# Reordering the opening and the first weight products of a fused FFT and GeGLU kernel on one core

## The chip, the core and the metric

The kernel runs on one core of a Trainium2 chip. The metric is device time in microseconds (us) of one execution, from the first to the last instruction that the device counts; the figure for the kernel before is the median of three runs. A profiled execution gives, beside that, the start and length of every instruction on each engine. Engine names: PE is the matrix engine (PEld its weight loads), DVE the vector engine, ACT the scalar engine, POOL the general engine, SP the engine that issues most DMA transfers. A name followed by q is the queue of that engine.

## The reference

For each of 8 sequences of 3008 tokens by 256 channels, take the real part of a two-dimensional Fourier transform, and send each of the 24064 resulting tokens through a gated feed-forward block of width 1536:

```python
X = np.fft.fft(x, axis=1)
X = np.fft.fft(X, axis=2)
y = X.real.astype(np.float32)           # (8, 3008, 256) -> (24064, 256)
g = y @ w_gate                          # 256 -> 1536
gelu = 0.5 * g * (1.0 + erf(g * inv_sqrt2))
val = y @ w_val
out = gelu * val @ w_out                # 1536 -> 256
```

## The kernel before, in words

**The mathematics in the code.** The transform over the sequence is split into two factors. A fold on symmetric pairs of rows (`fold_ops`, instructions at L221, L222, L225) fills `eo_sb`. Stage 1 (`s1`, L513, for batch 0; `s1t`, L555, for the others) multiplies `eo_sb` by a table of cosines and sines, `G`, into PSUM; the result is copied to `A_sb` (L519 on ACT, L521 on DVE). For batch 0 a transposing product (`ch`, L535) turns `A_sb` into `Z_sb` (copies at L541 and L543). Stage 2 (`tp_e` and `tp_o`, L591 and L596) multiplies `Z_sb` by `TP` and gives `E_sb` and `O_sb`, the even and the odd columns of the tokens (copies at L601 and L603); `tp_y` (L615) gives `EB_sb`, one column that is repeated over all partitions. A token t and its mirror token share these parts, so the output for both comes from one pair E, O.

The transform over the channels is not done on the data. It is multiplied into the weights: `make_w` (L451) multiplies the raw weights `w_raw` by a channel table `CW` and copies the product to `W_sb` (L457 on ACT, L459 on DVE). There are parts for gate and value, each even ("E") and odd ("O"), and a copy of the odd part times minus two ("M"; L466 on POOL, L468 on ACT, L470 on DVE) that turns a finished sum for t into the one for the mirror token.

**The blocks.** The work on tokens is cut into batches (8), token chunks (3 per batch, up to 512 tokens with as many mirror tokens) and slices of 128 of the 1536 hidden columns (12), which makes 288 blocks in one long list. A block's hidden slice is called fc. In each block the matrix engine issues: the gate product on E and on O (`l1_gate`, L674), the mirror gate of the block before (`l1_gate2`), the value product on E (`l1_value`), for the first chunk's first slices also on O, and the rest of the value product of the block before (`l1_value2`). ACT applies Gelu to both gate sums (L690 and L699), DVE and POOL form the products in `h_sb`. The second layer (`l2_piece`, L763) of a chunk is spread over the blocks of the next chunk.

**What sets the order.** Nothing is scheduled automatically: `opening()` and `feed()` record instructions, and each engine runs its own in that order. `plan()` gives two tables, `fill` and `pool`, that name by block number ("slot") which further pieces are recorded after the block's own work: `make_w`, the rest of batch 0's transform, the transform of the next batch, loads, and stores. A `make_w` in slot s makes columns that a block s + 1 or later needs: columns from 512 on are first used by block 4, columns from 1024 on by block 8.

**PSUM.** Each partition has eight tiles of 512 fp32 values, cut by tag: two "g", three "v", one "o", two "dft". A tag's tiles go round in turn, and a new matmul into a tile waits until the last reader of that tile has ended. In batch 0's opening `ps_any` takes "g", "v" and "dft" in turn. A block's gate sum occupies a "g" tile from its first matmul until its second Gelu.

**The opening.** It loads x, builds the tables, keeps the matrix engine busy with products of zeros (`warm(n)`: n matmuls of 128x512 into the "o" tile, L832), folds batch 0 on DVE, and runs stage 1, the first `make_w` and stage 2 for the first chunk. Then `feed()` begins with block 0.

The two lines that matter most for the order around block 0:

```python
tp_e(0, 0, 0, "A", tag="v")()     # even columns, copied by ACT
tp_e(0, 0, 1, "V", tag="v")()     # odd columns, copied by DVE
```

Of the kernel before, what the change touches and what calls it, by code (L numbers as in the profile page):

```python
# [11 lines left out]
AF = mybir.ActivationFunctionType  # L12
# [16 lines left out]
def kernel(  # L29
# [412 lines left out]

    V3_TO = 1024

    def make_w(i, f0, n, parts=(0, 1), engine="A", m_at=None, m_engine=None, tag="dft"):

        def run():
            ps = psum(tag)
# [7 lines left out]
            if engine == "A":  # L456
                nc.scalar.activation(dst, ps[:, :m], AF.Copy)  # L457
            else:
                nc.vector.tensor_copy(dst, ps[:, :m])  # L459
# [210 lines left out]
    def ffn_work(b):  # L670
# [5 lines left out]
        def cols_of(ci, fc):  # L676
# [3 lines left out]
                cstate[ci] = {"h": h_tile(), "ps": {}, "pso": {}}  # L680
            return n, c0, E, O, cstate[ci], slice(fc * 128, (fc + 1) * 128)

        def l1_gate(ci, fc):
            def run():
                n, _, E, O, st, fs = cols_of(ci, fc)
                pg = psum("g")
                mm(pg, n, "g", "E", fs, E, True, False)
                mm(pg, n, "g", "O", fs, O, False, True)
                gl = gelu_tile()
                nc.scalar.activation(gl[:, 0, :n], pg[:, :n], AF.Gelu)  # L690
                st["ps"][fc] = [pg, gl]
            return run
# [106 lines left out]
    def opening():  # L799
# [61 lines left out]
        s1(0, 2, 1)()  # L861
        t_sin()
        gelu_table()
        warm(8)
        fold_piece(5, 4)
        s1(0, 1, 0)()
        s1(0, 1, 1)()
        fold_piece(0, 1)
        s1(0, 3, 0)()
        s1(0, 3, 1)()  # L870
        fold_piece(1, 4)
        s1(0, 0, 0)()
        s1(0, 0, 1, "V")()
        minus = []
        make_w(0, 0, 256, m_at=minus, tag="o")()
        ch(0, 0, qs=(0,))()
        t_write()
        ch(0, 0, "V", qs=(1,))()
        ch(0, 1, qs=(0,))()
        ch(0, 1, "V", qs=(1,))()  # L880
        make_w(1, 0, 256, m_at=minus, m_engine="V", tag="g")()
        tp_e(0, 0, 0, "A", tag="v")()
        tp_e(0, 0, 1, "V", tag="v")()
        minus[0]()
        minus[1]()

# [2 lines left out]
    def plan():  # L889
# [6 lines left out]
        early = []  # L896
        for gi in (1, 2):
            e = "A" if gi == 1 else "V"
            early += [ch(0, 2 * gi), ch(0, 2 * gi + 1, e), tp_e(0, gi), tp_o(0, gi, e), tp_y(0, gi)]
        for s, f in (  # L900
                (0, make_w(0, 256, 256, m_engine="P")), (0, make_w(1, 256, 256, engine="V", m_engine="P")),
                (1, make_w(1, 512, 512, (1,), m_engine="P")), (1, lambda: load_wo(0)), (1, lambda: load_wo(1)),
                (2, make_w(0, 512, 512, (0,), "V")), (3, make_w(0, 512, 512, (1,))), (3, make_w(1, 512, 512, (0,), "V")),
                (4, make_w(1, 1024, 512, (1,), "V")), (5, make_w(0, 1024, 512, (0,), "V")),
                (5, make_yw()), (6, make_w(0, 1024, 512, (1,))), (6, tp_y(0, 0)), (7, make_w(1, 1024, 512, (0,), "V"))):
            at(fill, s, f)
        for i, f in enumerate(early):
            at(fill, (7, 8, 9, 10, 11, 12, 13, 14, 15, 16)[i], f)
# [141 lines left out]
```

## Time and profile before

| | |
|---|---|
| time, median of 3 runs | 618.9 us (618.87 to 619.16) |
| span of the profiled execution | 617.5 us |
| PE busy | 606.2 us, 98% |
| DVE busy | 575.7 us, 93% |
| POOL busy | 508.3 us, 82% |
| ACT busy | 425.5 us, 69% |
| first gate matmul of block 0 | starts 18.71 us after the span's start |
| last matmuls | one group of 12 from 611.99 us |
| granted clock of the matrix engine | mean 0.997; 0.50 in the half-microseconds from 10.5 to 13.5 us |

The profile is read from the top: the shares of busy time say which engine is full, the slices of the span say where it is not, the waits say what it waited for there, and the timeline of one engine gives the start and the length of each group of instructions, with the idle time ahead of it and what ended that in brackets. A matmul of 512 columns is listed with some 0.38 us from issue to result, while the next one starts 0.216 us later (21.43, 21.64 and 21.86 us are the starts of three in a row): lengths overlap, so steps from start to start are what the matrix engine's time is counted in. The starts of the first gate matmul on E of each block are a clock for the whole kernel. In the profile they are, for blocks 0 to 11: 18.71, 20.78, 22.64, 24.41, 26.56, 28.82, 31.02, 32.98, 35.65, 37.96, 39.79, 41.93 us.

### The profile page before, as it was taken

Reading aid. Unit: us, or ns where it says so; the run is one execution under the profiler, and the core shown is the slowest. Engines: PE = TensorE matmul, PEld = TensorE weight load, DVE = VectorE, ACT = ScalarE, POOL = GpSimd, SP = SyncE. Lnnn points to the kernel's source line nnn. Section 1 sums busy time; section 2 is a strip of 40 time slices with the busy share of each in tenths; the row PEclk is TensorE's granted clock in tenths of the full one; section 3 lists DMA queues with packets and bytes.
Section 4 is the critical chain, followed back from the end, with each engine's and each line's share of the span. In section 5 each row is a group of like instructions: output and inputs, shape, how many; then the busy total and the mean of one; then the engine's idle time right before and its main releaser. Section 6 shows DMA issues by size and latency. Waiting matters only on the chain.

```text
span 617.5 us, 12744 instructions
## 1 busy us (share of the span) xinstructions
PE 606.2 (98%) x4182; PEld 406.5 (66%) x4230; DVE 575.7 (93%) x940; ACT 425.5 (69%) x825; POOL 508.3 (82%) x513
## 2 busy tenths in 40 slices
PE   8999999999999999999999999999999999999997
PEld 4456666666666666666666666666666666666666
DVE  8789999999999999999999999999999999999992
ACT  6778767676776677767767677666776667666661
POOL 8889899999997999879997899969987555555561
PEclk8999999999999999999999999999999999999999
DMA  9961825546352464632653335543123232211123
GB/s 178 201 130 31 241 65 153 132 120 175 97 157 79 113 146 110 159 93 57 164 138 103 108 95 123 140 107 96 44 69 76 62 91 51 66 48 43 39 52 82
DMA packets 52466, 65.40 MB, mean 106 GB/s; under 512 B 7629, under 2 KB 47278, under 8 KB 50004
## 3 DMA queue, kind: packets, MB, share of 16 engines
q1 hardware_dynamic: 45472, 49.03, 30.5%
q0 software_dynamic: 6608, 15.29, 11.4%
q8 instruction: 33, 0.54, 0.4%
q10 hardware_dynamic: 320, 0.26, 0.2%
q14 instruction: 33, 0.27, 0.1%
HBM read 39.65 MB, written 30.17 MB: 113 GB/s over the span
## 4 chain that ended last, share of the span: by engine, by line
PE 94%; DMA 2%; issue 1%; DVE 1%; ACT 1%; SPq 0%; POOL 0%; DVEq 0%; POOLq 0%; ACTq 0%
PE ps_o L763 39%; PE ps_g L674 29%; PE ps_v L674 20%; PE ps_dft L555 2%; PE ps_dft L591 2%; DMA xb<-in_x_dram,idx 1%; DMA out_dram<-out_sb 1%; PE ps_o L832 1%; PE ps_dft L451 0%; DVE h_sb L730 0%; ACT A_sb L519 0%; PE ps_dft L535 0%; DVE W_sb L459 0%; SPq L668 0%; ACT out_sb L779 0%
## 5 line engine op out<-in xcount | busy, mean ns | idle before, releaser
L738 POOL TENSOR_TENSOR h_sb<-gelu_sb,v_sb 128x512 bf16<-128x512 bf16 (+1 forms) x280 | 319.6, 1146 | 89.5 <-DVE v_sb L736 76.6
L763 PE MATMUL ps_o<-Wo_sb,h_sb 128*128 128x256 bf16 (+1 forms) x2232 | 334.4, 272 | 0.0
L763 PEld LDWEIGHTS <-h_sb 128*128 128x128 bf16 (+1 forms) x2304 | 228.7, 100 | 111.3 <-POOL h_sb L738 1.0
L718 DVE SCALAR_TENSOR_TENSOR ve_sb<-EB_sb,yw,ps_v 128x512 f32<-128x512 bf16 (+1 forms) x280 | 206.3, 737 | 19.3 <-PE ps_v L674 16.6
L690 ACT ACTIVATE gelu_sb<-ps_g 128x512 bf16<-128x512 f32 (+1 forms) x288 | 169.3, 588 | 79.6 <-PE ps_g L674 64.8
L734 DVE TENSOR_TENSOR h_sb<-gelu_sb,ps_v 128x512 bf16<-128x512 bf16 (+1 forms) x280 | 189.8, 678 | 1.6 <-ACT gelu_sb L699 1.0
L674 PEld LDWEIGHTS <-W_sb 128*128 128x128 bf16 x1440 | 138.2, 98 | 79.3 <-issue 2.2
L736 DVE SCALAR_TENSOR_TENSOR v_sb<-ve_sb,ps_v 128x512 f32<-128x512 f32 (+1 forms) x280 | 187.5, 669 | 0.0
L699 ACT ACTIVATE gelu_sb<-ps_g 128x512 bf16<-128x512 f32 (+1 forms) x288 | 168.9, 586 | 0.0
L674 PE MATMUL ps_g<-O_sb,W_sb 128*128 128x512 bf16 (+1 forms) x530 | 159.1, 374 | 2.7 <-DVE O_sb L603 0.2
L674 PE MATMUL ps_g<-E_sb,W_sb 128*128 128x512 bf16 (+1 forms) x288 | 108.0, 375 | 0.7 <-ACT gelu_sb L699 0.3
L674 PE MATMUL ps_v<-E_sb,W_sb 128*128 128x512 bf16 (+1 forms) x287 | 107.6, 375 | 0.8 <-DVE W_sb L459 0.6
L674 PE MATMUL ps_v<-O_sb,W_sb 128*128 128x512 bf16 (+1 forms) x288 | 108.0, 375 | 0.1
L783 ACT ACTIVATE out_sb<-ps_o 128x512 f32<-128x512 f32 x92 | 54.9, 597 | 34.0 <-PE ps_o L763 33.7
L229 POOL TENSOR_TENSOR eo_sb<-ab_sb 94x512 bf16<-94x512 f32 (+1 forms) x70 | 77.6, 1111 | 0.4
L558 ACT ACTIVATE S_sb<-ps_dft 96x512 bf16<-96x512 f32 x56 | 33.1, 592 | 29.7 <-PE ps_dft L555 29.7
L222 POOL TENSOR_TENSOR ab_sb<-x_raw,x_raw 94x508 f32<-94x508 f32 (+1 forms) x30 | 33.0, 1100 | 0.0
L225 POOL TENSOR_TENSOR ab_sb<-x_raw,x_raw 94x508 f32<-94x508 f32 (+1 forms) x30 | 33.0, 1099 | 0.0
L555 PE MATMUL ps_dft<-eo_sb,G 94*96 94x256 bf16 x119 | 22.3, 272 | 0.0
L601 ACT ACTIVATE E_sb<-ps_dft 128x512 bf16<-128x512 f32 (+1 forms) x23 | 13.6, 589 | 11.9 <-PE ps_dft L591 11.9
L601 ACT ACTIVATE O_sb<-ps_dft 128x512 bf16<-128x512 f32 (+1 forms) x22 | 13.0, 590 | 11.6 <-PE ps_dft L591 11.1
L163 POOL DMA_INDIRECT x_raw<-in_x_dram,idx x18 | 17.2, 954 | 2.9 <-issue 0.8
(151 smaller groups left out, 207.7 us busy)
## 6 DMA issues: line engine op xcount, KB each, us to landing
out_dram<-out_sb SPq DMA_DIRECT2D x364, 64.0 KB
x_raw<-in_x_dram SPq DMA_DIRECT2D x10, 768.0 KB
Z_sb<-z SPq DMA_DIRECT2D x7, 768.0 KB
z<-S_sb SPq DMA_DIRECT2D x7, 576.0 KB
EB_sb<-yrow SPq DMA_DIRECT2D x6, 376.2 KB
z<-S_sb SPq DMA_DIRECT2D x7, 192.0 KB
x_raw<-in_x_dram SPq DMA_DIRECT2D x2, 640.0 KB
x_stage<-in_x_dram SPq DMA_DIRECT2D x1, 768.0 KB
```

The lines of the kernel that those rows point to most:

```text
L229: eng.tensor_tensor(_sub(eo, [[C, nj], [1, 128]], j0 * C + g * 128), ab(0, 0, [[1, 128]]), ab(1, 0, [[1, 128]]), op=op)
L555: nc.tensor.matmul(ps[:96, q * C : (q + 1) * C], G[:, j, :], _sub(eo, [[1, C]], j * C), start=(j == js[0]), stop=(j == js[-1]))
L558: nc.scalar.activation(_sub(st["S"], [[1, 512]], (4 * jg + 2 * half) * C, part_num=96), ps[:96, :], AF.Copy)
L674: nc.tensor.matmul(ps[:, :n], W[nm, part][:, fs], src, start=start, stop=stop, **kw)
L690: nc.scalar.activation(gl[:, 0, :n], pg[:, :n], AF.Gelu)
L699: nc.scalar.activation(_sub(gl, [[-1, n]], TOK + n - 1), pg[:, :n], AF.Gelu)
L718: nc.vector.scalar_tensor_tensor(ve[:, :n], EB_bufs[b][:, c0 : c0 + n], yw[:, fc : fc + 1], pv[:, :n], op0=ALU.mult, op1=ALU.add)
L734: nc.vector.tensor_tensor(st["h"][:, fc, 0, :n], gl[:, 0, :n], pv[:, :n], op=ALU.mult)
L736: nc.vector.scalar_tensor_tensor(_sub(vv, [[-1, n]], n - 1), ve[:, :n], 2.0, pv[:, :n], op0=ALU.mult, op1=ALU.subtract)
L738: nc.gpsimd.tensor_tensor(st["h"][:, fc, 1, :n], gl[:, 1, :n], vv[:, :n], op=ALU.mult)
L763: nc.tensor.matmul(pso[:m, half], st["h"][:, fc, sign, h0 : h0 + m], Wo_sb[:, fc, :], start=(fc == 0 and not (first and sign)), stop=(fc = ...
L783: nc.scalar.activation(_sub(osb, [[1, 2 * C]], 0, part_num=m), pso[:m, :], AF.Copy)
```

## The change

It has five edits, all before or around the first dozen blocks, but for the last.

1. *Stage 1's last copies.* `warm(8)` becomes `warm(6)`; the fold of the last piece is recorded ahead of stage 1's group (3), though on DVE's own queue its place does not move; a `warm(1)` is put in ahead of the last group; and the copy of `s1(0, 3, 1)` goes from ACT to DVE, so that ACT and DVE share the last ones.
2. *Weight copies behind the transposes'.* The matmuls of the two first `make_w` stay where they were, but their copies to `W_sb` are recorded later (a new argument, `copy_at`): the first one after ACT's copies of `Z_sb`, the second one after the copy of `E_sb`. The second `make_w` uses a "v" tile instead of a "g" tile, and the odd columns' sum a "dft" tile instead of a "v" tile.
3. *Two even gate halves ahead.* For batch 0 the even half of the gate product is issued for slices 0 and 1 before block 0's odd half.
4. *First weights sooner.* Some of the `make_w` in slots 2 to 7 move one or two slots forward; three products change the engine that copies or scales them (value even 512 and value even 1024 from DVE to ACT; the scaled copy of gate odd 1024 from ACT to DVE). `make_yw` and `tp_y(0, 0)` move one slot later, and the two copies of `Z_sb` in slots 7 and 8 swap engines.
5. *Rows a slot sooner.* The transfers that write `EB_sb` and row 0 of `O_sb` for batches 1 to 7 (`tp_rows`, L642) are recorded in the slot of the last product, not in the next one.

No matmul of the computation is added or taken away; there is one warm matmul fewer.

```diff
+            def copy():
+                if engine == "A":
+                    nc.scalar.activation(dst, ps[:, :m], AF.Copy)
+                else:
+                    nc.vector.tensor_copy(dst, ps[:, :m])
+            if copy_at is None:
+                copy()
             else:
-                nc.vector.tensor_copy(dst, ps[:, :m])
+                copy_at.append(copy)
...
+        ahead = {fc: gate_even(0, fc) for fc in range(2)} if b == 0 else {}
...
-                pg = psum("g")
-                mm(pg, n, "g", "E", fs, E, True, False)
+                pg = ahead.pop(fc) if b == ci == 0 and fc in ahead else gate_even(ci, fc)
                 mm(pg, n, "g", "O", fs, O, False, True)
...
-        warm(8)
+        warm(6)
         fold_piece(5, 4)
         s1(0, 1, 0)()
         s1(0, 1, 1)()
         fold_piece(0, 1)
+        fold_piece(1, 4)
         s1(0, 3, 0)()
-        s1(0, 3, 1)()
-        fold_piece(1, 4)
+        s1(0, 3, 1, "V")()
+        warm(1)
         s1(0, 0, 0)()
         s1(0, 0, 1, "V")()
-        minus = []
-        make_w(0, 0, 256, m_at=minus, tag="o")()
-        ch(0, 0, qs=(0,))()
+        minus, copies = [], []
+        make_w(0, 0, 256, m_at=minus, tag="o", copy_at=copies)()
         t_write()
-        ch(0, 0, "V", qs=(1,))()
-        ch(0, 1, qs=(0,))()
-        ch(0, 1, "V", qs=(1,))()
-        make_w(1, 0, 256, m_at=minus, m_engine="V", tag="g")()
+        for pp in range(2):
+            ch(0, pp, qs=(0,))()
+            ch(0, pp, "V", qs=(1,))()
+        copies.pop()()
+        make_w(1, 0, 256, m_at=minus, m_engine="V", tag="v", copy_at=copies)()
         tp_e(0, 0, 0, "A", tag="v")()
-        tp_e(0, 0, 1, "V", tag="v")()
+        tp_e(0, 0, 1, "V", tag="dft")()
+        copies.pop()()
...
-            early += [ch(0, 2 * gi), ch(0, 2 * gi + 1, e), tp_e(0, gi), tp_o(0, gi, e), tp_y(0, gi)]
+            early += [ch(0, 2 * gi, "V" if gi == 1 else "A"), ch(0, 2 * gi + 1, e), tp_e(0, gi), tp_o(0, gi, e), tp_y(0, gi)]
...
-                (2, make_w(0, 512, 512, (0,), "V")), (3, make_w(0, 512, 512, (1,))), (3, make_w(1, 512, 512, (0,), "V")),
-                (4, make_w(1, 1024, 512, (1,), "V")), (5, make_w(0, 1024, 512, (0,), "V")),
-                (5, make_yw()), (6, make_w(0, 1024, 512, (1,))), (6, tp_y(0, 0)), (7, make_w(1, 1024, 512, (0,), "V"))):
+                (2, make_w(0, 512, 512, (0,), "V")), (2, make_w(0, 512, 512, (1,))),
+                (3, make_w(1, 512, 512, (0,))), (4, make_w(1, 1024, 512, (1,), "V")),
+                (5, make_w(1, 1024, 512, (0,))), (5, make_w(0, 1024, 512, (0,), "V")),
+                (6, make_yw()), (6, make_w(0, 1024, 512, (1,), m_engine="V")), (7, tp_y(0, 0))):
...
-                    at(fill, s + 1, tp_rows(b, chunk_off[i // 2 - 1], chunk_len[i // 2 - 1]))
+                    at(fill, s, tp_rows(b, chunk_off[i // 2 - 1], chunk_len[i // 2 - 1]))
             if b > 1:
-                at(fill, s + 1, tp_rows(b, 0, HALF))
+                at(fill, s, tp_rows(b, 0, HALF))
```

More of the change, by code (lines that the diff above doesn't have):

```diff
@@ L443, with make_w @@
     V3_TO = 1024
-    def make_w(i, f0, n, parts=(0, 1), engine="A", m_at=None, m_engine=None, tag="dft"):
+    def make_w(i, f0, n, parts=(0, 1), engine="A", m_at=None, m_engine=None, tag="dft", copy_at=None):
         def run():
@@ L455, in run @@
             dst = _sub(W_sb, [[F, len(parts)], [1, n]], (2 * i + parts[0]) * F + f0)
-            if engine == "A":
-                nc.scalar.activation(dst, ps[:, :m], AF.Copy)
+            def copy():
[5 more added lines that the diff above has]
+                copy()
             else:
-                nc.vector.tensor_copy(dst, ps[:, :m])
+                copy_at.append(copy)
             if 1 in parts and (i == 0 or f0 < V3_TO):
@@ L681, in cols_of, with gate_even @@
             return n, c0, E, O, cstate[ci], slice(fc * 128, (fc + 1) * 128)
+        def gate_even(ci, fc):
+            n, _, E, _, _, fs = cols_of(ci, fc)
+            pg = psum("g")
+            mm(pg, n, "g", "E", fs, E, True, False)
+            return pg
+        ahead = {fc: gate_even(0, fc) for fc in range(2)} if b == 0 else {}
         def l1_gate(ci, fc):
```

## The prediction

> **What bounds the kernel now.** I read the page's busy slices and its chain first:
>
> ```profile
> PE   8999999999999999999999999999999999999997
> ...
> PE 94%; DMA 2%; issue 1%; DVE 1%; ACT 1%; SPq 0%; POOL 0%; DVEq 0%; POOLq 0%; ACTq 0%
> ```
>
> The matrix engine is full in every slice but the first and the last, and the chain is 94% its own. From the dozenth block on it runs through: of 606.2 us busy in a span of 617.5 us, what is missing lies in the opening, around the first blocks and in the tail. The change leaves the tail and the number of matmuls alone, so it can win only the waits between about 10 and 40 us, plus any later one. The matrix engine's waits (engine, line, who ended it: us in total, times, longest):
>
> ```profile
> PE ps_dft L535 <- ACT A_sb L519: 0.7, 1, 0.7
> PE ps_v L674 <- DVE W_sb L459: 0.6, 1, 0.6
> ...
> PE ps_g L674 <- ACT gelu_sb L699: 0.3, 1, 0.3
> PE ps_g L674 <- ACT E_sb L601: 0.3, 1, 0.3
> ...
> PE ps_g L674 <- DVE O_sb L603: 0.2, 1, 0.2
> ```
>
> Read in order of time: stage 1's copies (0.7), the even columns (0.3), the odd columns (0.2), then at 35 to 37 us a "g" tile still held by a second Gelu (0.3) and a weight copy on DVE (0.6). The view shows only waits longer than a matmul's overlap, so I also take the steps between block starts. Block 7 takes 2.67 us (32.98 to 35.65) for ten steps' worth of matmuls (6 x 0.216 own, 0.43 weights, 0.43 transposes: 2.16); block 8 takes 2.31 for 1.51 (5 x 0.216 + 0.43). So 0.51 + 0.80 = 1.3 us are lost there. Block 4 takes 2.26 for 1.73 (1.30 + 0.43): 0.5 us lost.
>
> The opening's chain is on ACT's timeline (start, length, what, idle time before):
>
> ```profile
> 13.04 0.20 ACT L426 ACTIVATE dump<-col 1x1 f32<-1x1 f32 x1
> 13.97 0.49 ACT L519 ACTIVATE A_sb<-ps_dft 128x384 bf16<-128x384 f32 x1 [0.73 <-PE ps_dft L513]
> ...
> 15.47 0.53 ACT L519 ACTIVATE A_sb<-ps_g 128x384 bf16<-128x384 f32 x1
> 15.84 0.65 ACT L457 ACTIVATE W_sb<-ps_o 128x512 bf16<-128x512 f32 x1
> ...
> 17.57 0.60 ACT L457 ACTIVATE W_sb<-ps_g 128x512 bf16<-128x512 f32 x1 [0.27 <-PE ps_g L451]
> 18.06 0.59 ACT L601 ACTIVATE E_sb<-ps_v 128x512 bf16<-128x512 f32 x1
> ```
>
> ACT is free at 13.24 but waits 0.73 us for stage 1, which stands behind the eight warm matmuls; five copies follow at 0.37 us each to 16.00; and the copy of E starts only when the weight copy lets ACT go. The matrix engine's timeline gives the other side:
>
> ```profile
> 10.25 3.37 PE L832 MATMUL ps_o<-gelu_sb 128*128 128x512 bf16 x8
> 13.41 0.52 PE L513 MATMUL ps_dft<-G,eo_sb 94*128 94x96 bf16 x4
> ```
>
> **What the Trainium skill says.** "TensorE: Matmul & The Clock Gate", Part 1: an idle engine runs at half clock, and a window of about 3.4 us of activity, running freely, lifts it. The trace agrees: eight warm matmuls take 3.16 us (0.395 each) against 0.216 later, and the granted clock is 0.50 from 10.5 to about 13.9 us, 3.4 us. The same page, "Back-to-back issue gap", prices 512 columns cold at N / 1.2 = 427 ns; my price for a removed warm one. Its "Architectural detail" has ACT and DVE strictly first in, first out; the trace's E copy behind the weight copy agrees. "PSUM — Partial Sum Buffer", "Specifications (TRN2)", gives 8 banks; the tags use 2 + 3 + 1 + 2, so moving a tile to another tag takes a turn from that tag. No view of this trace shows the banks.
>
> **Part by part.**
>
> *Stage 1.* Two cold warm matmuls less: 13.41 - 2 x 0.427 = 12.56 for `s1(0, 1, 0)`. Its input is there: DVE's fold L222 ended at 12.34, its L225 at 12.68, when the second group needs it. The result comes 0.52 later, 13.08, before ACT is free at 13.24; so ACT's first copy moves from 13.97 to 13.25. After that the matrix engine sets the pace. Four groups of 4, 4, 5 and 5 matmuls at 0.080 cold reach 13.92 with one left, the clock rises, then `warm(1)` 0.22 and eight at 0.043: 14.52, drained at about 14.70. DVE, free of folds since 13.90, copies group (3) from 14.15 and the last from 14.75 to 15.3; ACT's fourth copy ends about 15.05. The first transpose then starts at 15.35 instead of 16.05: -0.7. `t_write` (about 0.5 on DVE) ends by 15.8, before the first DVE copy of Z is ready, 15.9: free. The first weight matmuls lie in the wait before the transposes, as now.
>
> *Weight copies behind.* The last Z copy ended at 17.55, so 16.85 now; the fourth product of `tp_e` gives E at 17.1. On ACT the first weight copy runs 16.5 to 17.0, behind the Z copies, and the second is behind E, so E's copy starts at 17.15 where it now starts 0.91 later, and the first gate matmul at 17.8 against 18.71: -0.9. The second weight copy (17.65 to 18.25) and the scaled one (to 18.6) are needed at 18.7 and 20: hidden. O: its sum ended at 18.38, now 17.7; copy to 18.4, gate odd at 18.45 against 19.26: -0.8.
>
> *Halves ahead.* Block 1's even half (0.216) goes into the wait for O, 18.02 to 18.45, and block 1 is shorter by it: -0.2. Both "g" tiles are then held until block 0's second Gelu (from about 21), and ACT's Gelus queue behind a weight copy, which may cost 0.1 in block 2. At block 2: about -1.0.
>
> *First weights.* Block 2 now has two weight sums, so behind it ACT has a copy and a scaled copy (0.49 + 0.57) ahead of two Gelus (2 x 0.5). Block 2 starts at 21.6, its matmuls end 2.16 later, 23.9 with the drain; 23.9 + 2.06 = 26.0, and block 4's gate needs the "g" tile then freed. The matrix engine gets there at 21.6 + 2.16 + 1.73 = 25.5: a wait of 0.5 to 0.6 in place of the 0.5 that block 4 has now. So +0.1. Blocks 7 to 9: the value columns that block 8 waited for are made in slot 5 by ACT, two slots earlier: 0.6 gone. In slots 6 and 7 ACT lost the scaled copy (0.57, to DVE, which had 1.47 us idle before 35.14) and a Z copy, so the "g" tile is free in time: 0.4 gone. The Z copy back on ACT in slot 8 may cost block 9 some 0.2 to 0.3; DVE keeps its load. Net -1.0 of the 1.3.
>
> *Rows.* DVE waits once for these rows, and the block starts around it (95.46, 97.57, 99.52; 2.11 where 1.95 is clear) show what it costs the matrix engine:
>
> ```profile
> DVE ve_sb L718 <- DMA EB_sb<-yrow: 1.0, 1, 1.0
> ```
>
> A slot is 2 us, more than the 1.0: gone, worth -0.2. On SP's queue the transfer stands ahead of output stores, which nobody waits for here; its own row transfer waits for the copy of O just recorded.
>
> Sum: -0.9 - 0.2 + 0.1 + 0.1 - 1.0 - 0.2 = -2.1; for the drains that I rounded down, -2.0. 618.9 - 2.0 = 616.9 us.
>
> **The rivals.** (a) *Waits move on:* the "g" tiles and ACT's queue give back in blocks 2 to 9 what the weights win; only the opening and the rows are kept: -0.9 - 0.2 + 0.1 = -1.0, 617.9. For it: ACT is the releaser in two of the five waits; against: ACT is 69% busy. (b) *The clock rises a window later,* because stage 1's small matmuls count for less than warm ones: 2.4 us of matmuls between 13.9 and 17.3 take twice as long, of which about 1 hides in waits: +1.4, 618.3. Against: they stream 96 columns in 80 ns, without gaps. (c) *Slower:* two windows late, to 20.7: some 5.2 us of matmuls double, waits hide 1.5, so +3.7 - 2.0 = +1.7, 620.6. Nothing in the trace speaks for a whole second window. (d) *More:* block 4's wait vanishes too, and block 9 has none: -2.8, 616.1.
>
> **How the numbers follow.** Forecast 0.66, (a) 0.13, (b) 0.08, (c) 0.05, (d) 0.08. Both bounds of unknown costs (the warm price 0.395 or 0.427, block 4's and 9's wait 0.2 to 0.6 each) give the forecast 616.4 to 617.5. The range 616.2 to 618.0 takes in the forecast and (a), and leaves out (b), (c) and half of (d): 0.17. The bound of 0.2% is 1.24 us, 617.66: faster 0.66 + 0.08 + 0.04 of (a) = 0.78; same 0.17; slower 0.05.
>
> **What would show it.** ACT's first `A_sb` copy after the table load near 13.25; first transpose near 15.35; first gate matmul near 17.8, two even ones in a row; block 2 near 21.6; a wait on L699's tile at block 4 near 26; block 8 about 1.3 and block 10 about 1.9 earlier than now; no DVE wait for `EB_sb`; from there a constant distance to the end. A clock of 0.5 past 14 us, or waits of over 1 us in blocks 2 to 9, would make it wrong.

## The result and the profile after

The changed kernel takes 616.56 us (median of 4 runs, 616.33 to 616.80) against 618.95 us (4 runs, 618.87 to 619.16): a ratio of 0.9961, 95% interval 0.9944 to 0.9978, so 2.4 us less. The forecast was 616.9 us, 2.0 us less. The span of the profiled execution goes from 617.5 to 614.9 us.

The page of the changed kernel, busy tenths in 40 slices and the shares of the chain:

```profile
PE   8999999999999999999999999999999999999997
...
PE 94%; DVE 2%; issue 1%; DMA 1%; ACT 1%; SPq 1%; POOL 0%; DVEq 0%; POOLq 0%; ACTq 0%
```

Nothing is to be seen at this scale: the matrix engine is as full as before, and 2.6 us are a sixth of one slice. The waits of the matrix engine in the changed kernel (engine, line, who ended it: us in total, times, longest) say more:

```profile
PE ps_o L847 <- DVE col L316: 1.2, 1, 1.2
PE ps_g L681 <- ACT gelu_sb L714: 0.5, 1, 0.5
...
PE ps_g L681 <- DVE O_sb L610: 0.3, 1, 0.3
```

Of the waits shown of before, three are gone: the 0.7 for stage 1's copy `A_sb`, the 0.6 for a weight copy on DVE, the 0.3 for `E_sb`. The one for the "g" tile (second Gelu, now L714) has grown from 0.3 to 0.5, as the forecast had it, and it stands where the forecast put it, at block 4. The list of DVE's waits has no entry for `EB_sb` any more. The opening on ACT's timeline of the changed kernel (start, length, what, idle time before and its releaser):

```profile
12.55 0.20 ACT L426 ACTIVATE dump<-col 1x1 f32<-1x1 f32 x1
12.66 0.46 ACT L526 ACTIVATE A_sb<-ps_dft 128x384 bf16<-128x384 f32 x1
...
14.16 0.49 ACT L526 ACTIVATE A_sb<-ps_g 128x384 bf16<-128x384 f32 x1 [0.30 <-PE ps_g L520]
...
15.99 0.59 ACT L459 ACTIVATE W_sb<-ps_o 128x512 bf16<-128x512 f32 x1
16.67 0.60 ACT L608 ACTIVATE E_sb<-ps_v 128x512 bf16<-128x512 f32 x1
```

ACT's first copy follows the table load at once (before: 0.73 idle), four copies are on ACT where there were five, and the weight copy lies ahead of `E_sb` without delaying it. The same stretch on the matrix engine, with block 4:

```profile
9.87 2.31 PE L847 MATMUL ps_o<-gelu_sb 128*128 128x512 bf16 x6
11.96 0.53 PE L520 MATMUL ps_dft<-G,eo_sb 94*128 94x96 bf16 x4
...
15.07 0.38 PE L542 MATMUL ps_g<-II,A_sb 128*128 128x256 bf16 x2
...
17.32 0.38 PE L681 MATMUL ps_g<-E_sb,W_sb 128*128 128x512 bf16 x1
17.96 0.38 PE L681 MATMUL ps_g<-O_sb,W_sb 128*128 128x512 bf16 x1 [0.26 <-DVE O_sb L610]
...
25.58 0.38 PE L681 MATMUL ps_g<-E_sb,W_sb 128*128 128x512 bf16 x1 [0.51 <-ACT gelu_sb L714]
```

Block 0's even half now starts at 17.32 instead of 18.71. (The record of the second even half, at about 17.54, is missing from the trace; block 1 later starts with its odd products, so the half was issued. The trace of the opening alone, e2 below, has it: 17.70, behind the first one at 17.49.) Against before, the starts of the blocks come earlier by 1.38 us (block 0), 1.62 (2), 0.98 (4), 1.86 (8), 2.47 (10 to 28), 2.70 (from 38 on) and 2.55 at the end.

These starts count from the beginning of the span, and part of the difference isn't the change's: DVE's first fold (L221) starts at 8.26 us instead of 8.64. So I cut the span at events that both kernels have: the first fold; the second transposing product of the opening (`ps_g`, L535 before and L542 after); block 0's odd half; block 2; block 10; block 80; block 287. The experiments below rest on this table (us; each number is the difference of two starts on a timeline; the labels are those of the experiments below):

| kernel | first fold at | to 2nd transposing product | to odd half | to block 2 | to block 10 | to block 80 | to block 287 |
|---|---|---|---|---|---|---|---|
| before | 8.64 | 7.64 | 2.98 | 3.38 | 17.14 | 144.15 | 415.98 |
| before, e1 | 9.07 | 7.63 | 2.89 | 3.29 | 17.14 | 144.23 | 415.98 |
| after | 8.26 | 6.81 | 2.89 | 3.07 | 16.29 | 143.91 | 416.14 |
| after, e5 | 8.46 | 6.26 | 2.89 | 3.07 | 16.29 | 144.49 | 416.13 |
| e2 opening alone | 8.30 | 6.93 | 2.89 | 3.07 | 17.14 | 144.74 | 416.13 |
| e3 weights alone | 8.28 | 7.01 | 2.89 | 3.29 | 16.29 | 144.52 | 415.98 |
| e4 rows alone | 8.32 | 7.30 | 2.89 | 3.28 | 17.14 | 144.06 | 415.98 |
| e6 scaled copy on DVE | 8.57 | 7.76 | 2.89 | 3.07 | 15.80 | 143.91 | 415.99 |
| e7 eight warm ones | 8.26 | 6.33 | 2.88 | 3.07 | 16.29 | 143.91 | 416.15 |
| e8 copies first | 8.77 | 6.50 | 2.88 | 3.07 | 16.29 | 143.91 | 416.14 |
| e9 filled | 8.26 | 6.83 | 2.88 | 3.07 | 16.29 | 143.91 | 416.15 |
| e10 filled, scaled on DVE | 8.33 | 7.21 | 2.89 | 3.07 | 15.80 | 143.91 | 415.99 |
| e11 before, filled | 9.01 | 6.95 | 2.89 | 3.28 | 17.14 | 145.44 | 415.98 |
| e12 no half ahead | 8.41 | 6.65 | 2.89 | 3.29 | 16.29 | 143.92 | 416.12 |

Between the two profiles the change gains 0.83 us in stage 1, 0.31 from the odd half to block 2, 0.85 from block 2 to 10 and 0.24 from block 10 to 80. The rest (0.38 at the fold, 0.09 before the odd half, and 0.16 lost after block 80) is looked at below.

### The profile page after: what moved, and what is told of

It is laid out like the page before. It is cut to its first block, busy times and chain, and to the rows that moved or that the text cites. A ratio compares the mean times of both kernels' runs of the same rounds, so it can differ in the third digit from the quotient of the medians.

```text
span 614.9 us, 12747 instructions
## 1 busy us (share of the span) xinstructions
PE 605.4 (98%) x4181; PEld 406.9 (66%) x4229; DVE 577.3 (94%) x941; ACT 425.0 (69%) x824; POOL 508.9 (83%) x513
## 4 chain that ended last, share of the span: by engine, by line
PE 94%; DVE 2%; issue 1%; DMA 1%; ACT 1%; SPq 1%; POOL 0%; DVEq 0%; POOLq 0%; ACTq 0%
PE ps_o L778 39%; PE ps_g L681 29%; PE ps_v L681 20%; PE ps_dft L562 2%; PE ps_dft L598 2%; DMA out_dram<-out_sb 1%; PE ps_dft L451 1%; SPq L675 1%; PE ps_o L847 0%; PE ps_dft L542 0%; ACT gelu_sb L705 0%; ACT gelu_sb L714 0%; DVE v_sb L751 0%; POOL h_sb L753 0%; PE ps_dft L603 0%
## 5 line engine op out<-in xcount | busy, mean ns | idle before, releaser
L714 ACT ACTIVATE gelu_sb<-ps_g 128x512 bf16<-128x512 f32 (+1 forms) x288 | 168.6, 585 | 0.0
```

What stands on the lines that cost most here:

```text
L714: nc.scalar.activation(_sub(gl, [[-1, n]], TOK + n - 1), pg[:, :n], AF.Gelu)
```

## The experiments

### Before once more: is the earlier fold the change's?

The kernel before, unchanged, in a run of its own.

> The kernel before, unchanged, for a second profile. In the profile after, DVE's first fold of batch 0 (L222) starts at 8.35 us, in the one before at 8.74, though nothing ahead of it was changed. Theory L (that 0.39 us is chance: the landing of the first rows varies from execution to execution): this profile has the fold's start somewhere between 8.3 and 8.8 us, not at exactly 8.74, and the time is the same within 0.3 us. Rival D (the change itself makes the rows land sooner): fold at 8.74 again, within 0.05.

Measured: 619.24 us (14 runs) against 618.89 (67 runs), ratio 1.0006 (0.9992 to 1.0019). DVE's timeline in the unchanged kernel:

```profile
9.07 0.19 DVE L221 TENSOR_TENSOR eo_sb<-x_stage,xb 94x8 bf16<-94x8 f32 x1 [0.74 <-DMA xb<-in_x_dram,idx]
```

and in the changed one:

```profile
8.26 0.19 DVE L221 TENSOR_TENSOR eo_sb<-x_stage,xb 94x8 bf16<-94x8 f32 x1
```

The same program starts its first fold at 8.64 in one execution and at 9.07 in another, later than I had allowed for; over the 14 profiles of the table it is 8.26 to 9.07, and 8.28 and 9.07 are both from the old opening (e3 and e1). What ends the wait is the DMA of the first rows. So the 0.38 us is the landing of a transfer in that execution, and no part of the change. The repetition shows a second thing: 2.89 and 3.29 are the usual lengths of the next stretches, and the profile of before was 0.09 long in each.

### The parts of the change, each alone

Edits 1 to 3 alone (the changed kernel with these put back):

```diff
-                (2, make_w(0, 512, 512, (0,), "V")), (2, make_w(0, 512, 512, (1,))),
+                (2, make_w(0, 512, 512, (0,), "V")), (3, make_w(0, 512, 512, (1,))), (3, make_w(1, 512, 512, (0,), "V")),
...
-                at(fill, s, tp_rows(b, 0, HALF))
+                at(fill, s + 1, tp_rows(b, 0, HALF))
```

> Edits 1 to 3 alone (stage 1's copies, weight copies behind, two even halves ahead); the weights' slots and the rows as before. Theory T (each part takes away its own wait, and they add up): -1.0 us, 617.9: block 0 about 0.9 sooner than before at the same fold start, block 2 1.0 sooner, and the waits of blocks 4, 7 and 8 as before (0.5, 0.5, 0.8). Rival M (waits move on): the blocks' later waits grow by what the opening won, the sum is within 0.3 us of 618.9.

Measured: 618.46 us (22 runs) against 618.89, ratio 0.9986 (0.9976 to 0.9996). The matrix engine's waits with the opening alone:

```profile
PE ps_v L681 <- DVE W_sb L461: 0.6, 1, 0.6
PE ps_g L681 <- ACT gelu_sb L714: 0.3, 1, 0.3
...
PE ps_dft L634 <- DMA Z_sb<-z: 0.2, 1, 0.2
```

The two waits of blocks 7 to 9 are back, block 2 to 10 takes 17.14 as before; the opening itself is like that of the changed kernel (2.89, 3.07). In block 28 this execution also waited for a transfer into `Z_sb`, as one other (e5) did for 0.3 us; 144.74 from block 10 to 80 has that in it. By the medians the opening is worth 0.4 us and not the 1.0 expected; why, the repetition below shows.

Edit 4 alone (the kernel before, with this):

```diff
-                (2, make_w(0, 512, 512, (0,), "V")), (3, make_w(0, 512, 512, (1,))), (3, make_w(1, 512, 512, (0,), "V")),
-                (4, make_w(1, 1024, 512, (1,), "V")), (5, make_w(0, 1024, 512, (0,), "V")),
+                (2, make_w(0, 512, 512, (0,), "V")), (2, make_w(0, 512, 512, (1,))),
+                (3, make_w(1, 512, 512, (0,))), (4, make_w(1, 1024, 512, (1,), "V")),
+                (5, make_w(1, 1024, 512, (0,))), (5, make_w(0, 1024, 512, (0,), "V")),
...
```

> Edit 4 alone (slots and engines of the first weight products). Theory T: -1.0 us, 617.9: block 2 as before, block 4 0.5 later (one more product before it, and the wait for the second Gelu of block 2), block 8 0.3 sooner, block 10 0.9 sooner, no wait for a weight copy on DVE at block 8. Rival M: the new queue on ACT gives back at block 4 and 5 what block 8 wins: within 0.3 us of 618.9.

Measured: 618.15 us (22 runs) against 618.89, ratio 0.9990 (0.9980 to 0.9999). The matrix engine's waits with the weights alone:

```profile
PE ps_g L674 <- ACT gelu_sb L699: 0.5, 1, 0.5
PE ps_g L674 <- ACT E_sb L601: 0.3, 1, 0.3
```

The wait for the weight copy is gone and the one for the "g" tile has its new size, without any edit in the opening. Block 2 to 10 takes 16.29, as in every kernel that has edit 4 as it was made: in the profiles edit 4 is worth 0.85 us, in the medians 0.74, under the 1.0 expected.

Edit 5 alone (the kernel before, with `s` for `s + 1` in the two lines of `tp_rows`):

```diff
-                at(fill, s + 1, tp_rows(b, 0, HALF))
+                at(fill, s, tp_rows(b, 0, HALF))
```

> Edit 5 alone (rows recorded one slot sooner). Theory T: -0.2 us, 618.7: DVE's 1.0 us of waiting for EB_sb near 95 us is gone and the matrix engine's steps between blocks there go from 2.11 to 1.95 us twice. Rival H (hidden anyway): no change of time, under 0.1 us, since DVE had the slack.

Measured: 618.71 us (22 runs) against 618.89, ratio 0.9995 (0.9985 to 1.0004): by time alone, nothing can be said. The stretch from block 10 to 80 takes 144.06; in five profiles without edit 5 it takes 144.15 to 145.44, in nine with it 143.91 or 143.92 seven times, 144.06 and 144.49. Of the two things expected of its own profile one came: DVE's wait for `EB_sb` is gone. But block 37, whose 2.11 us (95.46 to 97.57) were to become 1.95, still takes 2.11 (94.55 to 96.65):

```profile
94.55 0.38 PE L674 MATMUL ps_g<-E_sb,W_sb 128*128 128x512 bf16 x1
...
96.65 0.38 PE L674 MATMUL ps_g<-E_sb,W_sb 128*128 128x512 bf16 x1
```

It is down to 1.95 only in the eight profiles whose kernels have edits 4 and 5 and the new opening, whole or nearly so. The 0.09 that the rows alone win in this stretch lies in block 36 (2.15 for 2.22). Later blocks say more about what the edit is for. Block 72, the first one of the third batch, takes 2.15 in all nine profiles with edit 5 and in that of before, but 2.24, 2.20, 2.36 and 3.11 in e1, e2, e3 and e11, the four others without it; in e11 its odd gate product waits 0.80 us for the row of `O_sb` (`O_sb<-yrow`). What the other three wait for there the waits do not list. So without edit 5 the rows can come too late for the matrix engine, and in none of the nine profiles with it do they.

SP's queue says how a slot helps. In the kernel before:

```profile
81.99 2.42 SPq L668 DMA_DIRECT2D out_dram<-out_sb  x4
...
88.14 2.38 SPq L668 DMA_DIRECT2D out_dram<-out_sb  x4
90.57 0.58 SPq L642 DMA_DIRECT2D EB_sb<-yrow  x1
```

In the kernel after:

```profile
79.51 2.41 SPq L675 DMA_DIRECT2D out_dram<-out_sb  x4
82.03 0.53 SPq L649 DMA_DIRECT2D EB_sb<-yrow  x1
...
85.66 2.40 SPq L675 DMA_DIRECT2D out_dram<-out_sb  x4
```

The four stores of one output tile take 2.4 us in both. Before, the rows stood behind the stores of two tiles, and between the two the queue did nothing from 84.4 to 88.14: the second tile was not there yet. ACT copies it just then:

```profile
87.52 0.60 ACT L783 ACTIVATE out_sb<-ps_o 128x512 f32<-128x512 f32 x1 [0.37 <-PE ps_o L763]
```

A slot earlier the rows stand ahead of that tile's stores, and miss both the 3.7 us of waiting for it and the 2.4 us of its stores. They leave 8.5 us sooner in the span, of which some 2.6 us are the lead that the changed kernel has by then; the other 5.9 us are nearly three slots, where I had counted on one of 2 us.

The three parts' medians sum to -0.43 - 0.74 - 0.18 = -1.35 us, where the whole change has -2.4. That gap was the open question after these runs, and the next one answers it.

### After once more: the clock at the opening

> The changed kernel, unchanged, timed together with the next three and with the kernel before. Theory T (own waits): 616.5 to 616.9, -2.0 to -2.4 us. In the profile the time from the first fold on DVE (start of the first L221) to block 0's gate is 9.0 to 9.2 us whatever the phase of the clock, since two of the six early profiles (e2 and after) have 9.18 and 9.06; with the old opening it was 10.06, 10.07, 9.73 and 9.44. Rival P (the gain of the first timing was mostly the luck of landing and clock): -1.4 us or less, the sum of the three parts as timed alone (-0.4, -0.7, -0.2).

Measured: 617.21 us (5 runs) against 619.08 (15 runs), ratio 0.9966 (0.9952 to 0.9979): 1.9 us less, between the two expectations. In this profile the granted clock does not fall at all in the opening, and fold to second transposing product takes 6.26 instead of 6.81, with the same program; fold to block 0's gate takes 8.51, not the 9.0 to 9.2 that was to hold whatever the clock does. Wherever a trace shows half clock in the opening, it lasts 3.41 us or twice that, so I cut the opening into stretches of 3.41 us, counted from the first entry of the trace's clock record (us, PE busy and number of instructions, granted clock, DMA share, GB/s), first in this repetition:

```profile
5.50:8.91 3.41, 2.64 (x17) 1.00 1.11 219
8.91:12.33 3.42, 2.27 (x18) 1.00 1.15 194
```

and in the first profile of the changed kernel:

```profile
6.91:10.33 3.42, 2.92 (x25) 1.00 1.06 192
10.33:13.74 3.41, 3.41 (x24) 0.50 1.21 167
```

The edges fall at other moments of the opening from one execution to the next; here the clock stays, there it falls for one stretch. The mean granted clock that each run reports tells which it was: one stretch of 3.41 us at half clock takes 0.5 x 3.41 / 615 = 0.003 off it. Sorting all runs of the kernel before that lie beside the experiments (and e1's) by it gives 50 runs with 0.999 or 1.0, mean 618.35 us; 76 with 0.996 or 0.997, mean 619.39; 7 with 0.993 or 0.994, mean 621.25. (A run of it at 0.998, and one of the changed kernel, are left out.) So runs of the kernel before with one stretch at half clock are 1.0 us longer, with a second one 1.9 more. Nothing on record tells beforehand which a run will meet. Comparing like with like (difference of means to the kernel before with as many stretches; in brackets the interval of 95% from resampling the runs; runs of all experiments pooled, since the kernel before has nearly the same means beside each group of experiments: 618.25 to 618.36 without a stretch, 619.25 to 619.51 with one):

| | no stretch | one stretch |
|---|---|---|
| e2 opening alone | -0.03 (-0.72 to 1.11), 3 runs, of which one at 619.49 | -0.83 (-1.15 to -0.46), 17 runs |
| e3 weights alone | -0.71 (-0.93 to -0.49), 5 runs | -0.73 (-1.13 to -0.27), 16 runs |
| e4 rows alone | -0.51 (-0.70 to -0.30), 5 runs | -0.33 (-0.64 to -0.01), 16 runs |
| the whole change (with e5) | -1.55 (-1.89 to -1.23), 4 runs | -2.20 (-2.63 to -1.77), 4 runs |

With one stretch the parts sum to -1.89 us, inside the interval of the whole; without one to -1.25, inside it too. So nothing speaks against the parts adding up, though the intervals are wide. The sum of medians fell short because each median mixed the clock's cases in another proportion: 3 of the opening's 22 runs had no stretch, 26 of the 67 beside them. And the whole change is worth less where the clock stays up. That would fit the opening, from which warm matmuls at half clock were taken away, but its three runs are too few to show it.

### Does it matter that the weight copies stand behind? Does the half ahead?

Both weight copies back where they were on ACT, all else as after:

```diff
-        make_w(0, 0, 256, m_at=minus, tag="o", copy_at=copies)()
+        make_w(0, 0, 256, m_at=minus, tag="o")()
...
-        copies.pop()()
-        make_w(1, 0, 256, m_at=minus, m_engine="V", tag="v", copy_at=copies)()
+        make_w(1, 0, 256, m_at=minus, m_engine="V", tag="v")()
```

> The changed kernel with both first weight copies back ahead on ACT: the first before the Z copies, the second before E's copy. Theory T (the copy of E waits for ACT behind the second weight copy): first fold to block 0's gate 0.2 us longer than the changed kernel's 9.06 to 9.18, and the time 0.1 to 0.2 us over it, since the odd columns' copy on DVE bounds block 0 just after. Rival S (nothing of it reaches the odd columns): block 0's gate later, but its odd half and all that follows at the same time, and the time the same within 0.1 us.

Measured: 617.54 us (9 runs) against 619.08, ratio 0.9971 (0.9960 to 0.9982); with one stretch at half clock it is 2.04 us under the kernel before (1.78 to 2.33, 8 runs), where the whole change is 2.20 under. The matrix engine with the copies first:

```profile
17.69 0.38 PE L681 MATMUL ps_g<-E_sb,W_sb 128*128 128x512 bf16 x1 [0.33 <-ACT E_sb L608]
18.15 0.38 PE L681 MATMUL ps_g<-O_sb,W_sb 128*128 128x512 bf16 x1
```

The wait of 0.33 for `E_sb` is back, as before the change. But the odd half starts 2.88 us after the second transposing product, and block 2 3.07 later, both as in the changed kernel. The odd half waits for `O_sb`, which DVE copies, and DVE's chain from the transposing product to it is not touched by the order on ACT: 2.88 or 2.89 in all profiles but the first one of before. What the later copies save ahead of the even half is waited for ahead of the odd half: in the profile moving them is worth nothing, and the runs, 2.04 against 2.20, don't tell the two orders apart. (The tiles' tags, the rest of edit 2, stayed as in the changed kernel here, and were not tried apart.)

The half-product ahead taken out, all else as after:

```diff
-        ahead = {fc: gate_even(0, fc) for fc in range(2)} if b == 0 else {}
+        ahead = {}
```

> The changed kernel without edit 3: each even gate half directly ahead of its odd half. Theory T (block 1's even half fills the wait for the odd columns): from the first transpose to block 2 it takes 0.2 us longer than in after (6.32), 6.5, and 0.2 us in all, 616.8 to 617.4. Rival G (two g tiles held early cost as much on ACT as the filled wait brings): 6.3 again, no difference.

Measured: 617.22 us (8 runs) against 618.86 (38 runs), ratio 0.9976 (0.9965 to 0.9986). The odd half to block 2 takes 3.29 instead of 3.07: edit 3 is worth 0.22 us, one matmul's 0.216. The table agrees: 3.28 or 3.29 in every other profile without the half ahead, but for the 3.38 of the first one of before, and 3.07 in every one with it. The matrix engine without it:

```profile
17.32 0.38 PE L681 MATMUL ps_g<-E_sb,W_sb 128*128 128x512 bf16 x1
17.95 0.38 PE L681 MATMUL ps_g<-O_sb,W_sb 128*128 128x512 bf16 x1 [0.26 <-DVE O_sb L610]
```

Between the two the engine stands for 0.42 us (0.63 less 0.216); the half ahead fills 0.216 of it.

### What do the two warm matmuls cost?

```diff
-        warm(6)
+        warm(8)
...
-        warm(1)
```

> The changed kernel with eight warm matmuls in the second loop again and without the single one later. Theory T (two cold warm matmuls stand before stage 1): the time from the first fold to block 0's gate is 0.4 to 0.5 us longer, 9.5 to 9.6, when the loop runs at half clock, and only 0 to 0.2 longer when the clock falls late, as in e3 (at 10.77 us, so that the loop's first four run at full clock); the time is 0.2 to 0.4 us over the changed kernel's. Rival C (the warm matmuls are needed to raise the clock): not slower, and the clock rises a window sooner than with six.

Measured: 616.81 us (5 runs) against 619.08, ratio 0.9958 (0.9945 to 0.9972). The profile fell into an execution whose clock did not fall, as did four of the five runs, so the case that the question was about, half clock, was not met. At full clock the eight take 1.89 us:

```profile
9.86 1.89 PE L847 MATMUL ps_o<-gelu_sb 128*128 128x512 bf16 x8
```

0.236 each, and fold to second transposing product is 6.33 against 6.26 in the repetition of the changed kernel. So at full clock edit 1's smaller warm-up is worth no more than 0.07; for half clock this run is inconclusive. What stands for half clock are three pairs in the table whose edges lie alike, each an old opening and a new one: before and after (the clock falls 1.86 and 2.07 us after the first fold), 7.64 to 6.81; the rows alone and the copies first (it falls 0.68 and 0.69 after it), 7.30 to 6.50; and the weights alone and the opening alone (2.49 and 2.46 after it, so that the warm matmuls run partly at full clock), 7.01 to 6.93. Edit 1 is worth 0.1 to 0.8 us according to where the edges fall. How much of that is the smaller warm-up and how much the shared copies was not separated, and what the old opening takes where the clock stays up by itself, no profile shows.

### Can block 4's wait be taken away too?

The scaled copy of gate odd 512 in slot 2 goes from ACT to DVE:

```diff
-                (2, make_w(0, 512, 512, (0,), "V")), (2, make_w(0, 512, 512, (1,))),
+                (2, make_w(0, 512, 512, (0,), "V")), (2, make_w(0, 512, 512, (1,), m_engine="V")),
```

> The changed kernel with one more edit: the scaled copy of slot 2's weights (gate odd 512) is made by DVE, not by ACT. Theory T (block 4's wait of 0.51 us is ACT's queue of copy, scaled copy and two Gelus): the wait is gone or under 0.15, block 5 starts 0.4 us sooner against block 2 than in the profile after (27.35 - 21.03 = 6.32 there, 5.9 here), and it stays so: 0.4 us faster than the changed kernel. Rival M (waits move on): DVE, which takes 0.75 us more, holds a value tile longer, and block 5 comes no sooner.

Measured: 616.74 us (6 runs), beside which the changed kernel has 617.21 (e5); ratio to before 0.9954 (0.9940 to 0.9968). Block 2 to 10 takes 15.80 instead of 16.29, and the list of waits has none for block 4's gate product:

```profile
25.74 0.59 PE L451 MATMUL ps_dft<-w_raw,CW 128*128 128x512 bf16 x2
26.27 0.38 PE L681 MATMUL ps_g<-E_sb,W_sb 128*128 128x512 bf16 x1
```

DVE had room for it: 0.49 us are won, nearly the whole of the wait of 0.51, in both profiles that have this edit (e6 and e10). The opening of this execution was a bad one: the clock stayed at half for two stretches, 8.99 to 15.81 (same view as above):

```profile
5.58:8.99 3.41, 2.60 (x17) 1.00 1.09 212
8.99:12.40 3.41, 2.90 (x13) 0.50 1.14 191
12.40:15.81 3.41, 3.41 (x32) 0.50 1.25 165
```

Its fold to second transposing product takes 7.76, 0.95 more than in the first profile of after. Its six runs still have the lowest median of the four kernels that ran beside each other there, though the intervals of the ratios overlap; the two of them without a stretch at half clock are at 615.67 and 615.86, the four of the changed kernel without one at 616.34 to 617.21.

### Can the fall of the clock be kept away?

Twelve more warm matmuls in the gap ahead of stage 1, which from about 8 to 9 us is empty:

```diff
         columns = t_columns()
+        warm(12)
```

> The changed kernel with twelve more warm matmuls after the five small ones (t_columns) at 7.7 us, where the matrix engine otherwise waits for the first fold. Theory K (the clock falls because the engine idles 1 to 3 us before stage 1, and edits 1 and 2 are worth much only while it is down): the clock does not fall after its first rise, and the time from the first fold to block 0's gate is 8.5 to 8.6 us as in e5 and e7, whose clock stayed up, not 9.06, 9.18 or 10.02 as in after, e2 and e6 (8.9 at most if the twelve run cold and stage 1 waits for them); 616.3 to 616.8, and less scatter than the changed kernel's 616.3 to 617.7. Rival N (the fall has nothing to do with the idle stretch): the clock falls in some executions as before, gate at 9.0 or later, and the time is no better.

Measured: 617.16 us (12 runs) against 618.86, ratio 0.9977 (0.9968 to 0.9985), above the 616.3 to 616.8 expected. None of the 12 runs shows a stretch at half clock (all have 0.999 or 1.0, where of the 38 runs of the kernel before beside them 21 are at 0.997 or lower). But ACT's timeline shows what that costs:

```profile
10.74 0.49 ACT L526 ACTIVATE A_sb<-ps_g 128x384 bf16<-128x384 f32 x1 [0.48 <-PE ps_g L520]
...
11.82 1.28 ACT L426 ACT_TABLE_LOAD   x1
```

The first product of stage 1 stands behind the twelve, starts at 10.36 instead of 9.09 in the first profile of the changed kernel (the first fold is at 8.26 in both), and pushes ACT's copies, and with them the table load, from 11.26 to 11.82. Fold to second transposing product is 6.83, against 6.26 for the changed kernel when its clock stays up by itself. Among runs without a fall it is 1.03 us under the kernel before, the changed kernel 1.55: there the filling costs some 0.5 us. It is no better on the whole (ratio 0.9977, where the changed kernel had 0.9961 and 0.9966), though the two were not timed side by side.

The same filling with the scaled copy on DVE:

> The same, and the scaled copy of slot 2's weights on DVE as in e6. Theory T and K together: e9's opening, and 15.8 us from block 2 to block 10 where the changed kernel has 16.29, so 0.5 us under e9: 615.8 to 616.3, the fastest of all. Rival: the opening's luck covers the 0.5 (no difference from e9 within 0.2).

Measured: 616.50 us (6 runs), ratio 0.9967 (0.9955 to 0.9979), 0.66 under the filled kernel beside it, again with 15.80 from block 2 to 10, but above the 615.8 to 616.3 expected. Its opening takes 7.21, longer than e9's 6.83: here the twelve start at 8.22, not at 7.76, and hold stage 1 up until 10.82, so what the filling costs varies too. And the filling in the kernel before:

> The kernel before with the same twelve warm matmuls and nothing else. Theory K: with the clock up, eight warm matmuls take 1.7 us instead of 3.2, so stage 1 no longer stands behind them, and the old opening is only about 0.1 us longer than the new one: first fold to block 0's gate 8.6 to 8.9 us instead of 10.06, about 618.0, up to 0.9 us faster than the kernel before. Rival T (edits 1 and 2 win their 0.9 us whatever the clock does): 9.4 or more, as in e3 (9.44), whose clock was down for one window.

Measured: 619.46 us (22 runs), ratio 1.0011 (1.0003 to 1.0019): slower. All its 22 runs have 0.999 or 1.0. The opening is shorter by 0.7 (6.95 against 7.64), but fold to block 0's gate takes 9.38 us, not the 8.6 to 8.9 expected, and this profile waits elsewhere:

```profile
PE ps_g L674 <- DMA O_sb<-yrow: 1.0, 2, 0.8
```

This is the row transfer that edit 5 brings forward; block 10 to 80 takes 145.44. Whether the filling makes the rows late more often, and is slower for that, was not tried. A shorter filling, of six or so, that leaves stage 1 free was not tried either.

## Why the prediction was right, step by step

The time, 616.56, lies 0.3 us under the forecast and inside its range, and the order of the sizes held. That it lies so near is in part luck: the second timing gave 1.9 us less in place of 2.4, like compared with like the change is worth 2.20 or 1.55 us according to the clock, and below two terms hit their size by errors that cancel or for another reason than the one given. The steps, by events that don't depend on the landing of the first rows:

**Stage 1, -0.7: low by 0.1 to 0.25.** The first copy of ACT comes 4.40 us after the first fold instead of 5.33, -0.93 where I had -0.72: I let it start at the end of the last instruction of the table load, while such starts overlap (12.55 with a length of 0.20, then 12.66), and ACT itself was 0.1 us further on. (The 0.395 us of a warm matmul that I read off was a mean of two clocks: in the trace of before the eight start 0.22, 0.38 and then 0.43 us apart, so the 0.427 that I priced with was right.) The second transposing product comes 0.83 earlier, the first one 0.95. The argument (two warm matmuls less, then ACT's own freedom is the limit, then the shared last copies) is what the timelines show. That the size, 0.1 to 0.8, depends on where the clock's edges fall was not in it.

**Weight copies behind, a further -0.2 at the even half, none of it at the odd one: worth nothing.** I wrote that E's copy starts when ACT lets it go, which is so (16.67, and not delayed), and booked -0.9 for the first gate matmul as if block 0 began with it. But I also wrote that the odd half comes 0.8 earlier, as stage 1 and DVE let it; that is the later of the two, and only it counts. The sum should have had -0.8 here, not -0.9. e8 showed it.

**Halves ahead, -0.2: right,** 0.22 in every pair. The 0.1 that it might cost in block 2 didn't come.

**First weights, +0.1 and -1.0: right, block 9 apart.** Block 2 to block 5 takes 6.32 instead of 6.18 (+0.14), block 5 to 7 4.36 instead of 4.16 (+0.20, with a weight product moved into it), block 7 to 10 5.61 instead of 6.81 (-1.20): -0.86 in all, forecast -0.9. The wait of 0.5 to 0.6 at block 4 is there with 0.51. The Z copy on ACT that was to cost block 9 some 0.2 to 0.3 did not: block 9 takes 1.77 instead of 1.83. That cost rested on a misreading of the change: the two copies of `Z_sb` in slots 7 and 8 do not swap engines. Before, both are on ACT (35.45 and 38.16 us); the change moves the first one to DVE (34.41) and leaves the second on ACT (35.50), so ACT only loses a copy.

**Rows, -0.2: the number is right in the profile of the pair (-0.24), the way to it is not.** I read the cost off block 37, 2.11 where 1.95 is clear, as DVE's wait for `EB_sb`. With the rows alone that wait is gone and block 37 takes 2.11 still (e4); so the 0.16 that it wins in the whole change is not the rows' alone, and 0.09 in e4's own profile is. What the edit is worth lies in executions in which the rows are late, as at block 72; the sorted runs put it at 0.3 to 0.5. I also counted one slot, 2 us; the rows come out of SP's queue some 5.9 us sooner, since they no longer wait for an output tile that isn't there yet and its stores.

**The sum.** -0.83 (stage 1) - 0.22 (halves) - 0.85 (weights) - 0.24 (rows) = -2.14 us, and 0.16 back after block 80 (below): -1.98, against -2.0 forecast and -2.20 (-2.63 to -1.77) measured among runs with one stretch at half clock, the case that the profile of before shows and that all my cold prices came from. In executions without it the change is worth 1.55, and no step of the forecast had that. Up to the transposes I had 0.13 too little and for the weight copies 0.2 too much; the two nearly cancel by chance, -0.9 forecast and -0.83 measured.

**The rivals.** (a), the waits move on and blocks 2 to 9 give everything back, is refuted by the 16.29 of the weights alone. (b) and (c), the clock rises one or two windows later, do occur: e6 lost a second stretch. But it is met by the kernel before as well (7 of 133 sorted runs) about as often as by the kernels with the new opening and no filling (4 of 59), so it isn't what the change does. (d), block 4's wait vanishes too, did not happen by itself; it takes one word in the plan, and is e6.

**Open.** Block 80 to 287 takes some 0.15 us more (416.12 to 416.15 for 415.98) in all seven profiles that have the new opening without the scaled copy on DVE, and in none of the other seven; so it comes with the opening's edits and is not chance; taking out the half ahead (e12), going back to eight warm matmuls (e7) or to the copies first (e8) leaves it as it is. It comes in single steps of 0.16 us: with the same matmuls, block 152 takes 2.11 us from start to start before and 1.95 after, blocks 123 and 270 take 1.95 before and 2.11 after. Block 37's step is of the same size and may be of the same kind. No step of mine had this, and what moves it isn't settled. Nor is it which activity keeps the clock from falling.

## What to carry to other kernels

An engine that is released earlier wins only up to the next thing its consumer waits for: where two halves are needed, price the change at the later one. When the parts of a change don't sum to the whole, look for a variable of the execution (here the granted clock's edges and the landing of the first transfer), sort the runs by it, and compare stretches between events inside the kernel rather than times from the start. A transfer that is issued "a slot sooner" on a queue can gain several slots, when what it jumps over is itself waiting for its data: look for the pauses inside a merged line of stores before calling it the time of the stores.

## What the runs showed of the hardware that I had not expected

- The edges of the clock's stretches of 3.41 us lie at different moments of the same program: 10.50, 10.92 and 9.00 us for the first fall in three profiles with the same opening (before, e1, e4), none at all in two profiles of unfilled openings of the changed kind. "TensorE: Matmul & The Clock Gate", Part 1, in the Trainium skill, has the engine go to half clock after at least one idle window; here it fell after a stretch with the matrix engine busy for 0.77 of 3.41 us (e1), but also after one with 2.92 of 3.42 (after), and stayed up after one with 2.27 of 3.42 (e5). So the page's condition doesn't describe these cases, and the busy time of the profile doesn't tell whether the clock will fall. Of the 40 runs with twelve filling matmuls (e9, e10, e11) none has a mean clock under 0.998.
- Runs of the kernel before with one stretch at half clock were 1.0 us longer on average, with a second one 1.9 us more. That the first stretch lies over warm matmuls and waits and the second over work would explain it, and the new opening fits (fold to second transposing product 6.26, 6.81 and 7.76 us with none, one and two, in e5, after and e6), but no profile shows the kernel before with two.
- SP's queue kept to the recorded order: in the kernel before a row transfer went out at 90.57 us, behind four stores that had waited from 84.4 to 88.14 us for their tile, and at 82.03 us where it was recorded ahead of them. A group of four stores itself held the queue for 2.4 us.
- DVE's first fold, which waits for the transfer of the first rows, started 8.26 to 9.07 us after the start, in kernels that are the same up to there but for twelve matmuls in three of them.
